# Eight small moves per batch in an attention and gated-convolution kernel: DMAs, or copies by GpSimd and VectorE

## The chip, the cores and the metric

One core of one Trainium2 chip. The time is the device time of one execution in microseconds (us). Most executions of one kernel agree closely; some fall into a slower state, which shows as runs more than 1.5% above the fastest of the same kernel. Such runs are left out of every ratio, but the medians quoted keep them. Ratios are the mean time of one kernel's fast runs over the mean of the other's fast runs in the same rounds on the same chip, so they are not quite the ratio of the medians that are quoted beside them. An interval is 95%.

## The reference

Eight batches, eight heads, 576 positions, head dimension 64. Attention is causal in blocks of 64; its result goes through a gated unit with a causal convolution over five positions.

```python
scores = q @ k.T / sqrt(64)                      # masked where block(i) < block(j)
attn   = exp(scores - max) / (sum + 1e-9)
x      = attn @ v                                # heads side by side: (8, 576, 512)
gate   = sigmoid(sum_k conv_w[k] * x shifted)    # five taps
out    = (gate * (x @ w_val)) @ w_out
```

## The kernel before

The kernel computes everything transposed, heads in pairs. Step `t` of the main loop holds the scores of one pair of heads of batch `t // 4`; older batches are interleaved with it. The denominators of a batch are summed by matmuls into one PSUM tile `dn`, head by head in rows of 32 partitions, and inverted in one instruction. The rows of `ri` then have to reach other partitions: a stream shuffle broadcasts one row within each group of 32 partitions (a quadrant), so each quadrant of `rq` first needs the rows of its own head, for both halves of the columns. `spread` does that with eight moves per batch.

```python
def den(b):
    dn = psG.tile([128, 9, 32], fp32, tag="G")
    ...                                                     # 69 to 72 matmuls
    ri = rp.tile([128, 288], fp32, tag="ri")
    nc.vector.reciprocal(out=ri[:, :], in_=dn[...])         # L257; L255 after the change

def spread(b):
    ri = ris.pop(b)
    for h in range(2):
        for u in range(2):
            for e in range(2):
                r0, r1 = 32 * (2 * h + u), 32 * (2 * h + e)
                move = nc.scalar.dma_start if b == 0 and h == 0 else load   # load: SyncE's queue
                move(out=rqs[b % 2][r0:r0 + 4, e, :], in_=ri[r1:r1 + 4, :])

def pv(t):
    rb = rp.tile([128, 2, 9, 32], fp32, tag="rb")
    nc.vector.stream_shuffle(out=rb[...], in_=rqs[b % 2][...], mask=[n] * 32)
    ...                                                     # x = v^T p, then xb = x * rb

def trans(hb, part):                                        # q and k of a later batch
    tr = psG.tile([128, 6, 128], fp16, tag="G")
    ...                                                     # six transposes by TensorE
    nc.vector.tensor_copy(out=qkT[b][...], in_=tr[...])     # L149; L147 after the change

def project(u, j):
    ot = psG.tile([128, 512], fp32, tag="G")                # four matmuls, then ob, then out
    ...
```

`psG` is a pool of four PSUM buffers that `dn`, `x`, `cv`, `tr`, `vp` and `ot` share in turn, so `ot` can start only when the `tr` four allocations earlier has been copied out. And only the matmuls and the loads are kept in program order; on VectorE, ScalarE and GpSimd a scheduler decides at build time in which order the instructions stand, and each engine then works through its list strictly in order.

The softmax here doesn't subtract the row's maximum and nothing guards it: scores larger than these inputs give would overflow.

## Time and profile before

| | before |
|---|---|
| median at first (3 runs, lowest to highest) | 257.14 us (255.12 to 259.04) |
| profiled execution, span | 255.2 us |
| TensorE busy | 219.8 us (86%), idle 31.4 us |
| VectorE, ScalarE, GpSimd busy | 57%, 54%, 36% |
| shuffles waiting for the small DMAs | 14.3 us in six places |

The busy line, the waits and the chain of one batch are shown in the prediction. The reading to keep: TensorE is the bound, so only idle time of TensorE can be won or lost; and in each batch there is a place where TensorE waits for two copies of `qkT` by VectorE with almost nothing to spare. The group of the projection's matmuls shows how small that wait is: after the bar, 144 matmuls had 0.5 us of idle time ahead of them in all.

```profile
L43 PE MATMUL ot<-w_out_sb,gv 128*128 128x512 f16 x144 | 35.8, 380 | 0.5
```

### The profile page before, as it was taken

The numbers are of one execution on the slowest core, as the hardware profiler recorded it, in microseconds if no ns is written. First come the engines' busy times: TensorE is split into PE (matmuls) and PEld (weight loads), VectorE is DVE, ScalarE is ACT, GpSimd is POOL, SyncE is SP. The second block draws the span as 40 slices with busy tenths as digits, with TensorE's granted clock in tenths as the row PEclk, the third lists the DMA queues.
The fourth block names the chain that finished last, engine by engine and source line by source line (L and its number), as shares of the span: only waits on it lengthen the run. The fifth ranks groups of instructions, "written<-read, shape, count | busy, mean of one in ns | idle before, by whom it ended". The sixth has DMA issues, their size and how long they took to land.

```text
span 255.2 us, 7299 instructions
## 1 busy us (share of the span) xinstructions
PE 219.8 (86%) x3064; PEld 152.2 (60%) x3064; DVE 145.8 (57%) x293; ACT 138.4 (54%) x233; POOL 92.4 (36%) x110
## 2 busy tenths in 40 slices
PE   0597869767999899999899989999999998999993
PEld 0374636645776467855675568655675567677661
DVE  2379952952787438652876457853766166366230
ACT  2459866255643675477554775376656761432533
POOL 7363963863943951454209240620027000000000
PEclk9999986798999999999999999999999999999999
DMA  6998787977398597059800992047101200230305
GB/s 190 342 298 203 247 231 150 300 242 184 100 286 183 184 355 188 5 154 383 229 5 11 356 296 69 7 148 205 44 4 47 92 33 4 89 125 3 154 13 205
DMA packets 25386, 40.62 MB, mean 159 GB/s; under 512 B 2053, under 2 KB 11525, under 8 KB 25354
## 3 DMA queue, kind: packets, MB, share of 16 engines
q1 hardware_dynamic: 20128, 30.69, 41.6%
q10 hardware_dynamic: 5226, 9.47, 9.9%
q8 instruction: 24, 0.39, 0.7%
q14 instruction: 8, 0.07, 0.1%
HBM read 30.42 MB, written 9.44 MB: 156 GB/s over the span
## 4 chain that ended last, share of the span: by engine, by line
PE 56%; ACT 18%; DVE 9%; issue 5%; DMA 5%; SPq 5%; ACTq 1%; DVEq 0%
PE cv L43 16%; ACT pt L178 15%; PE vp L43 9%; PE ps L43 8%; PE ot L43 7%; PE x L43 6%; PE dn L43 5%; PE tr L142 5%; SPq L46 5%; DVE qkT L149 4%; DVE ri L257 3%; DMA st<-in_k_dram 2%; ACT ob L366 2%; DMA rq_70<-ri 1%; DMA rq_71<-ri 1%
## 5 line engine op out<-in xcount | busy, mean ns | idle before, releaser
L178 ACT ACTIVATE pt<-ps 128x1024 f16<-128x1024 f32 (+1 forms) x96 | 76.0, 828 | 22.4 <-PE ps L43 19.5
L149 DVE COPY qkT<-tr 128x768 f16<-128x768 f16 (+1 forms) x62 | 49.2, 833 | 45.2 <-PE tr L142 45.1
L43 PE MATMUL ps<-qkT 64*64 64x64 f16 (+10 forms) x608 | 49.4, 253 | 17.7 <-ACT pt L178 14.2
L43 PEld LDWEIGHTS <-qkT 64*64 64x64 f16 (+1 forms) x608 | 24.7, 104 | 45.3 <-issue 38.1
L108 POOL CAST t<-st 128x1152 f16<-128x1152 f32 x30 | 34.3, 1145 | 33.3 <-DMA st<-in_q_dram 15.3
L338 ACT ACTIVATE th<-cv 128x288 f32<-128x288 f32 x64 | 26.1, 410 | 32.4 <-PE cv L43 30.8
L121 POOL CAST t<-st 128x2304 f16<-128x2304 f32 x8 | 16.9, 2106 | 67.2 <-PE x L43 50.8
L366 ACT COPY ob<-ot 128x512 f32<-128x512 f32 x36 | 21.3, 591 | 36.7 <-PE ot L43 33.3
L355 DVE SCALAR_TENSOR_TENSOR gv<-th,vp 128x288 f16<-128x288 f32 x64 | 26.8, 444 | 20.4 <-PE vp L43 19.9
L43 PE MATMUL ot<-w_out_sb,gv 128*128 128x512 f16 x144 | 35.8, 380 | 0.5
L43 PEld LDWEIGHTS <-diag 128*128 128x128 f16 x320 | 29.4, 98 | 10.0 <-issue 0.5
L142 PE MATMUL tr<-ident_59,t 128*128 128x128 f16 x288 | 26.9, 237 | 8.5 <-DVE ident_59 L82 6.7
L43 PE MATMUL x<-pt,t 128*64 128x256 f16 (+3 forms) x384 | 27.4, 255 | 2.7 <-DVE ri L257 2.0
L142 PEld LDWEIGHTS <-t 128*128 128x128 f16 x288 | 21.1, 106 | 12.4 <-DVE t L108 6.5
L204 ACT ACTIVATE pt<-ps 128x512 f16<-128x512 f32 x32 | 19.7, 615 | 15.0 <-PE ps L43 15.0
L43 PEld LDWEIGHTS <-w_val_sb 128*128 128x128 f16 x256 | 24.3, 98 | 5.4
L43 PEld LDWEIGHTS <-t 128*64 128x64 f16 x384 | 18.5, 112 | 6.7 <-issue 4.0
L43 PEld LDWEIGHTS <-gv 128*128 128x128 f16 x144 | 12.7, 97 | 14.8 <-issue 2.1
L257 DVE RECIPROCAL ri<-dn 128x288 f32<-128x288 f32 x8 | 15.7, 1958 | 8.3 <-PE dn L43 8.3
L43 PE MATMUL cv<-xb_67,diag 128*128 128x288 f16 x120 | 18.0, 299 | 0.2 <-DVE gv L355 0.2
L43 PE MATMUL cv<-xb_68,diag 128*128 128x288 f16 x120 | 16.8, 286 | 0.0
L43 PE MATMUL dn<-pt,oh 128*32 128x160 f16 (+7 forms) x704 | 14.1, 238 | 1.9 <-DVE xb_67 L316 1.9
(54 smaller groups left out, 223.5 us busy)
## 6 DMA issues: line engine op xcount, KB each, us to landing
st<-in_q_dram SPq DMA_DIRECT2D x32, 288.0 KB
st<-in_k_dram SPq DMA_DIRECT2D x32, 288.0 KB
out_dram<-ob ACTq DMA_DIRECT2D x36, 256.0 KB
st<-in_moe_w_val_dram SPq DMA_DIRECT2D x2, 512.0 KB
st<-in_moe_w_out_dram SPq DMA_DIRECT2D x2, 512.0 KB
rq_71<-ri SPq DMA_DIRECT2D x32, 4.5 KB
rq_70<-ri SPq DMA_DIRECT2D x28, 4.5 KB
st<-in_v_dram SPq DMA_DIRECT2D x8, 0.2 KB
```

Source lines behind the costliest of these rows:

```text
L43: tc.keep_in_program_order(nc.tensor.matmul(**kw))
L46: tc.keep_in_program_order(nc.sync.dma_start(**kw))
L108: cast(out=t[:, :, :, :], in_=st[:, :, :, :].rearrange("p z c d -> p c z d"))
L121: nc.gpsimd.tensor_copy(out=t[:, :, :], in_=st[:, :, :])
L142: tc.keep_in_program_order(nc.tensor.transpose(out=tr[:, s, :], in_=q16[hb, w][:, c, :, :], identity=ident16[:, :]))
L149: evac(out=qkT[b][:, 2 * half:2 * half + 2, w, :].rearrange("p n (x c) -> p n x c", c=9)[:, :, :, c0:c0 + len(ss)], in_=tr[:, ss[0]:ss[-1] ...
L178: nc.scalar.activation(out=pt[:, o:o + w], in_=src, func=AF.Exp, bias=0.0, scale=0.125)
L204: nc.scalar.activation(out=pt[:, 2048:2560].rearrange("p (h x) -> p h x", h=2), in_=ps[:, :, 0:256], func=AF.Exp, bias=0.0, scale=0.125)
L257: nc.vector.reciprocal(out=ri[:, :], in_=dn[:, :, :].rearrange("p j x -> p (j x)"))
L338: nc.scalar.activation(out=th[:, HF * hf:HF * hf + HF], in_=cv[:, :], func=AF.Tanh, bias=0.0, scale=0.5)
L355: nc.vector.scalar_tensor_tensor(out=gvs[u][:, g, c0:c0 + HF], in0=th[:, HF * hf:HF * hf + HF], scalar=1.0, in1=vp[:, :], op0=ALU.add, op1 ...
L366: nc.scalar.copy(out=ob[:, :], in_=ot[:, :])
```

## The change

The intent is to take the fixed cost of a DMA out of the path from reciprocal to shuffle: an on-chip copy of a whole quadrant moves the same rows. In batch 0 four of the eight are by VectorE; all others are by GpSimd. The memset of `rq` goes, as the copies now fill it.

```diff
-    for rq in rqs:
-        nc.gpsimd.memset(rq[:, :, :], 1.0)
...
-                    move = nc.scalar.dma_start if b == 0 and h == 0 else load
-                    move(out=rqs[b % 2][r0:r0 + 4, e, :], in_=ri[r1:r1 + 4, :])
+                    move = nc.vector if b == 0 and h == 0 else nc.gpsimd
+                    move.tensor_copy(out=rqs[b % 2][r0:r0 + 32, e, :], in_=ri[r1:r1 + 32, :])
```

## The prediction

> **What bounds the kernel now.** I read the page first: the engines, then the slices. TensorE is busy 86% and no other engine passes 57%.
>
> ```profile
> PE 219.8 (86%) x3064; PEld 152.2 (60%) x3064; DVE 145.8 (57%) x293; ACT 138.4 (54%) x233; POOL 92.4 (36%) x110
> ...
> PEclk9999986798999999999999999999999999999999
> ```
>
> The gaps of TensorE sum to 31.5 us, of which 9.4 lie before 12 us (first loads and casts). The rest are mostly repeated gaps of 0.41 us on the double-buffered score tiles, which this change does not touch. Three gaps look related to it: 1.65 us at 34.7, 1.88 us at 44.6, and 0.6 us in excess of the usual 0.41 at 84.0. So at most some 4 us can be won; the waits for the DMAs in the second fence are far larger in sum, but most of them are waits of an engine that is not the bound. The low PEclk digits (half clock in three stretches between 47 and 71 us) cost about 7 us and are not the change's business.
>
> Then the waits, for what the moved reciprocals hold up:
>
> ```profile
> DVE qkT L149 <- PE tr L142: 45.1, 23, 5.0
> ...
> POOL t L121 <- PE x L43: 50.8, 4, 22.3
> ...
> DVE rb L278 <- DMA rq_70<-ri: 8.5, 3, 3.6
> ...
> DVE rb L278 <- DMA rq_71<-ri: 5.8, 3, 3.4
> ```
>
> The shuffle (rb) waits 14.3 us in six places for the small DMAs: VectorE stands still there. GpSimd has long idle times: it runs ahead with its casts and waits for buffers.
>
> Last the chain of waits in one steady batch (the denominators of batch 5), which shows where VectorE is on the path:
>
> ```profile
> 157.28 1.56 PE dn L43 x70
> 158.85 0.02 issue
> 158.87 1.97 DVE ri L257
> 160.84 0.04 issue
> 160.88 0.64 PE x L43 x12
> 161.52 1.34 PE cv L43 x10
> 162.86 0.35 PE tr L142 x6
> 163.21 0.02 issue
> 163.24 0.52 DVE qkT L149
> 163.75 0.08 issue
> 163.83 0.72 DVE qkT L149
> 164.55 0.05 issue
> 164.59 1.05 PE ot L43 x4
> ```
>
> The output projection (ot) starts 0.05 us after the second qkT copy ends: it needs the PSUM buffer of the transposes, four allocations back in a pool of four. TensorE's previous work ends at 164.51, so there is only 0.08 us of slack: whatever delays these two copies delays TensorE.
>
> **What the Trainium skill says.** "GPSIMD Engine Reference", section 3.1: a simple GpSimd body runs at 1.03 cycles an element. The trace agrees: casts of 256, 1152 and 2304 columns took 398, 1145 and 2106 ns, which is 0.834 ns an element (1.00 cycle at 1.2 GHz) plus some 184 ns. The record alone misleads: "Perfetto Trace Analysis", section GPSIMD Engine Instruction, advises the spacing of starts. Consecutive 256-column casts start 0.345 us apart though each is recorded as 0.404, so the fixed part in a row is about 0.13 us. "DMA: Bandwidth & Descriptors", section on the anatomy of one DMA, gives about 2.0 us of fixed cost to a DMA, mostly the receipt of the write. The chain has 1.66 and 2.30 us from the last issue to the landing, plus 0.62 us for each issue. "Advanced Engine Details and Errata", Mode Summary: GpSimd and VectorE block each other when the Vector instruction uses both ports. The trace agrees: the 128x128 scalings (L379) took 238 ns alone and 1054 to 1281 ns when a GpSimd cast was running. The shuffles are not touched (800 ns without and 810 with GpSimd).
>
> **The change part by part.**
>
> *Removed:* 64 DMAs, 60 on SyncE's queue and 4 on ScalarE's, and two GpSimd memsets (1.2 us, at the start, where GpSimd then waits 4.67 us for the first load: nothing won). With the ScalarE DMAs go 0.58 to 0.70 us of issue each at 31.7 to 35.3 us. The exponential that TensorE waits for at 34.7 then starts about 1.1 us sooner (its scores are complete at about 34.3, it began at 35.31). With the SyncE DMAs goes the wait of 3.30 us of VectorE at 41.2 to 44.5, and TensorE's 1.88 us at 44.6 behind it. SyncE's loads no longer queue behind DMAs that wait for a reciprocal (7.4, 10.7 and 7.7 us blocked), but no TensorE gap after 12 us is put down to a late load, so I count nothing. At 83.5 us an output DMA on ScalarE's queue is held while the small DMAs are in flight; 0.6 us may go with them.
>
> *Added on VectorE, batch 0 only:* four 32x288 copies. They read and write SBUF in fp32, so they may use both ports, and at 33.8 us GpSimd is in the weight scaling (to 34.46) and then in its own four copies. I expect each to wait for the end of a GpSimd instruction: the four last some 1.9 us in place of about 0.9. VectorE has gaps of 0.94, 1.84 and 1.37 us there, so I charge 0.5 us.
>
> *Added on GpSimd:* 60 copies of 32x288. By the figures above one costs 184 + 288 x 0.834 = 424 ns by itself and 131 + 240 = 371 ns in a row; eight in a row take 7 x 0.371 + 0.424 = 3.02 us, plus 0.05 us for the semaphore: 3.07. That is 60 x 0.371 = 22 us more of GpSimd, which goes from 36% to some 44%: it does not become the bound. The casts behind the copies have slack of several steps of about 7 us.
>
> *Moved:* this decides it. Compared engine by engine, the instruction order of TensorE is the same, but on VectorE the scheduler has pulled the first shuffle of batches 2 to 6 ahead of the two qkT copies shown above (it stood five instructions later, and both shuffles together). VectorE works in order, so these copies now wait for eight GpSimd copies and a shuffle. For batch 5: the reciprocal ends at 160.83, the copies start at 160.88, end at 163.95, the shuffle starts at 163.98, and the next instruction 0.70 later (the spacing seen between two shuffles) at 164.68, in place of 163.24: 1.44 us late. The slack is 0.08 and existing waits of 0.05 remain, so TensorE loses about 1.4 us. Later in the batch VectorE gets this back (no wait of 1.07 us and one shuffle fewer at 167), but TensorE has no idle time there to return it. Batches 3, 4 and 6 have the same 2.40 us between the end of the reciprocal and the qkT copy; batch 2 has 2.6, so 1.2 us.
>
> *Sum:* 4 x 1.45 + 1.2 = +7.0 us; head -1.1 - 1.9 - 0.6 + 0.5 = -3.1 us. Batch 7 has the same hoist before its gating products: shuffle until 218.6 against a product that began at 217.42, 0.25 us late for a convolution at 219.95, but 0.19 us saved at 223.66: zero. Net +3.9 us on 257.14: **261.0 us**.
>
> **The rivals.**
> 1. *The win of the head and nothing else.* For it: the shuffles wait 14.3 us for DMAs, and a chain of eight issues (5 us) plus 2 us becomes 3.1 us. If the qkT copies had slack, or the GpSimd copies were done in under 1.7 us, the time would be 253 to 255 us. Against: the qkT copies end 0.05 us before the projection starts.
> 2. *GpSimd copies dearer than casts.* Nothing in this trace moves data between quadrants on GpSimd, and none has 32 partitions. At 0.55 us each a batch loses 1.3 us more: 5 x 1.3, so 267 us. Against: the cost fits columns alone, for 64 and for 128 partitions.
> 3. *GpSimd late for its copies,* because they stand behind casts that wait for loads and buffers, or the casts late behind the copies. Then transposes starve: some us more, 263 to 270. Against: GpSimd waits 7.7 to 22 us for a buffer in each batch from batch 3 on, and its queue reaches the copies with nothing open.
> 4. *VectorE and GpSimd share a port:* if shuffles were held by the copies, 32 x 0.4 us of VectorE. Against: 800 and 810 ns.
>
> **Range and chances.** The per-batch loss rests on a copy's spacing: 0.30 to 0.48 us gives a loss of 0.9 to 2.2 us, so +4.5 to +11 for five batches; the head gives -1.5 to -5. Runs of before spread from 255.1 to 259.0, and the half-clock stretches may fall elsewhere (2 us). That gives 256 to 266 us. The 2% line lies at 262.3, just above my value: slower by over 2% 0.37, within 2% 0.58, faster 0.05.
>
> **What would show it right or wrong.** Right: TensorE has a new gap of 1.2 to 1.6 us before ot in each of batches 2 to 6, put down to qkT, and just before it VectorE waits about 3 us less the x products for GpSimd's rq copies; the gaps at 34.7 and 44.6 us shrink; GpSimd is busy 112 to 118 us, the copies at 0.37 us spacing; the six waits of rb for DMAs are gone. Wrong: no gap before ot (then rival 1, the loss was hidden), copies at a spacing far from 0.37 us, the shuffle released by something other than rq, or the head unchanged because the VectorE copies or the load for the next transposes take the place of the waits removed.

## The result, and the profile after

The changed kernel is correct and slower: median 268.19 us (266.93 to 269.18, four runs) against 258.08 us (255.12 to 259.04, four runs, the upper two slow); ratio 1.047 (1.036 to 1.058). Repeated (run 10), the ratio was 1.039 (1.034 to 1.044). The predicted 261.0 us was too low, and the range of 256 to 266 us did not hold it.

The page of the changed kernel, engines and granted clock by slice:

```profile
PE 222.3 (84%) x3064; PEld 152.8 (58%) x3064; DVE 147.8 (56%) x297; ACT 138.7 (52%) x233; POOL 116.5 (44%) x168
...
PEclk9999988999897999999999999999999999999999
```

The span went from 255.2 to 265.1 us. TensorE's busy time grew by 2.5 us, its idle time from 31.4 to 38.9 us. GpSimd is at 44%, as predicted, and is no bound.

The waits of the changed kernel (engine and line, what released it: us in total, times, longest) name the place:

```profile
DVE rb L276 <- POOL rq_71 L267: 12.6, 4, 5.5
...
PE ot L43 <- DVE qkT L147: 10.5, 5, 2.1
...
DVE rb L276 <- POOL rq_70 L267: 7.1, 3, 2.4
...
PE x L43 <- DVE qkT L147: 3.5, 3, 2.6
...
PE ot L43 <- DVE gv L353: 1.3, 1, 1.3
```

The projection now waits five times, 10.5 us in all, each time for a `qkT` copy. The shuffles' waits for DMAs are gone, but they are not smaller: 12.6 + 7.1 = 19.7 us for GpSimd in place of 14.3 us for DMAs. The last two lines are waits of TensorE that the prediction did not have.

The chain of waits in the same batch as in the prediction (batch 5):

```profile
163.59 1.97 DVE ri L255
165.56 0.04 issue
...
167.46 0.42 POOL rq_71 L267
...
168.86 0.44 POOL rq_71 L267
...
169.33 0.03 DVE rb L276 x2
...
170.02 1.28 DVE qkT L147 x2
171.30 0.05 issue
171.34 1.05 PE ot L43 x4
```

The mechanism is the predicted one: copies, shuffle, `qkT`, `ot`. Its size is not. From the end of the reciprocal to the `qkT` copy there are 170.02 - 165.56 = 4.46 us; before it was 2.40. The copies start 0.46 us apart (at 167.46, 167.92, 168.39 and 168.86; two of them are in the cut), not 0.37, and the row of eight takes 3.67 us from 165.61 on, not 3.02.

TensorE issues the same 3064 matmuls in the same order in both kernels. So the start of the k-th matmul can be subtracted between two traces, and the difference shows where time is lost. This table, worked out so from the traces of the kernels named, gives the time lost against before (negative: won) in each stretch; the times are those of the kernel before, and the last four columns belong to experiments below.

| stretch of before | after | after again (run 10) | order pinned (run 1) | head alone (run 5) | one quadrant (run 9) |
|---|---|---|---|---|---|
| to 60.9 us: head, batch 0 | -4.62 | -2.45 | -5.91 | -4.35 | -4.13 |
| to 79.0: batch 1 | +3.13 | +1.45 | -0.22 | +1.87 | +1.49 |
| to 92.0: batch 2 | +2.15 | +2.33 | +1.60 | -0.58 | +1.56 |
| to 208.7: batches 3 to 6 | +8.13 | +10.66 | -0.03 | -0.02 | +6.16 |
| to the end: batch 7 | +1.12 | +1.12 | -0.35 | +0.03 | +0.46 |
| sum | +9.91 | +13.11 | -4.91 | -3.05 | +5.54 |

Each column is one profiled execution, and the clock of TensorE has a part in the first three rows. Up to the same matmul (60.9 us of before) the profile of before had 13.65 us at half clock, the others between 3.41 (after) and 13.65 us (run 9). And half clock in batch 1 shows in its row: in runs 2, 4, 7, 9 and 10 a stretch of it began between 59.3 and 61.5 us, and all five lose 1.44 to 1.49 us there; where none fell there and no gap opened (runs 1, 3, 6 and 8), 0.2 us is won.

In the changed kernel batches 3 to 6 lose 2.03, 2.04, 2.03 and 2.04 us, with no other difference between those matmuls: the gap of 2.12 us less the 0.08 us that was there before.

Batch 1 is another story. VectorE (start, duration, what, and in brackets the idle time before it and its releaser):

```profile
56.12 0.81 DVE L353 SCALAR_TENSOR_TENSOR gv<-th,vp 128x288 f16<-128x288 f32 x2
62.38 0.01 DVE L276 LOAD_MASK_SELECT rb<-rq_71  x1 [5.46 <-POOL rq_71 L267]
```

and GpSimd in the same time:

```profile
56.34 1.14 POOL L106 CAST t<-st 128x1152 f16<-128x1152 f32 x1
57.43 1.81 POOL L267 COPY rq_71<-ri 32x288 f32<-32x288 f32 x4
59.30 1.14 POOL L106 CAST t<-st 128x1152 f16<-128x1152 f32 x1
60.51 1.83 POOL L267 COPY rq_71<-ri 32x288 f32<-32x288 f32 x4
```

The reciprocals of batch 1 were ready at 48.33 us. GpSimd came to the copies at 57.43, after a row of casts and weight scalings without a break since 50.8, and put one more cast between the two halves. VectorE stood 5.46 us before the shuffle, both shuffles had been placed ahead of the `qkT` copies here, and TensorE lost 2.61 us at 62.5.

### The profile page after: what moved, and what is told of

Its sections match the earlier page's. It is cut to its first block, busy times and chain, and to the rows that moved or that the text cites.

```text
span 265.1 us, 7252 instructions
## 1 busy us (share of the span) xinstructions
PE 222.3 (84%) x3064; PEld 152.8 (58%) x3064; DVE 147.8 (56%) x297; ACT 138.7 (52%) x233; POOL 116.5 (44%) x168
## 4 chain that ended last, share of the span: by engine, by line
PE 60%; ACT 15%; DVE 8%; issue 6%; POOL 6%; DMA 3%; SPq 1%; POOLq 0%; ACTq 0%; DVEq 0%
PE cv L43 14%; ACT pt L176 12%; PE ps L43 11%; PE ot L43 9%; PE vp L43 9%; PE x L43 7%; PE tr L140 5%; PE dn L43 5%; DVE qkT L147 5%; DVE ri L255 3%; POOL rq_70 L267 3%; POOL rq_71 L267 3%; DMA st<-in_k_dram 2%; ACT ob L364 2%; DMA out_dram<-ob 1%
## 5 line engine op out<-in xcount | busy, mean ns | idle before, releaser
L43 PE MATMUL ps<-qkT 64*64 64x64 f16 (+10 forms) x608 | 51.2, 264 | 12.7 <-ACT pt L176 10.0
L43 PE MATMUL ot<-w_out_sb,gv 128*128 128x512 f16 x144 | 37.0, 388 | 12.0 <-DVE qkT L147 10.5
L140 PE MATMUL tr<-ident_59,t 128*128 128x128 f16 x288 | 27.6, 241 | 8.3 <-DVE ident_59 L82 6.4
L267 POOL COPY rq_71<-ri 32x288 f32<-32x288 f32 x32 | 13.5, 423 | 36.8 <-DVE ri L255 35.6
L267 POOL COPY rq_70<-ri 32x288 f32<-32x288 f32 x28 | 12.0, 427 | 32.9 <-DVE ri L255 31.9
L43 PEld LDWEIGHTS <-t 128*64 128x64 f16 x384 | 19.1, 113 | 10.4 <-issue 4.8
L43 PE MATMUL cv<-xb_67,diag 128*128 128x288 f16 x120 | 16.8, 286 | 0.0
```

Source lines behind the costliest of these rows:

```text
L43: tc.keep_in_program_order(nc.tensor.matmul(**kw))
L140: tc.keep_in_program_order(nc.tensor.transpose(out=tr[:, s, :], in_=q16[hb, w][:, c, :, :], identity=ident16[:, :]))
L267: move.tensor_copy(out=rqs[b % 2][r0:r0 + 32, e, :], in_=ri[r1:r1 + 32, :])
```

## The experiments

Theories at the start. A: the loss is the place of the shuffle in VectorE's list; the copies by themselves do no harm. B: the copies themselves, on GpSimd, disturb VectorE, the loads or the casts, wherever the shuffle stands. C: the copies are dearer than predicted, and the place is only the lever. A and C can both be partly true, so the tests of order come first, then those of the pace. Medians of before were 256.09 us in the first four runs and 257.33 in the next four, both on one chip, and 256.84 in the last two, on another.

**1. The order of before, the copies of after.** An ordering edge places each batch's shuffles behind the instruction that they followed before. Compared list by list, VectorE's order is then that of before, apart from the four copies of batch 0; the other engines have the order of the changed kernel.

```diff
...                                       # `last` notes each qkT copy and gating product
-        nc.vector.stream_shuffle(...)
+        behind = {1: (6, 2), 7: 23}.get(b, (2 * b + 3, 2))   # a qkT copy; in batch 7 a gating product
+        with tc.issue_after(last[behind].ins) if b else ExitStack():
+            nc.vector.stream_shuffle(...)
```

> The changed kernel with one thing undone: the shuffles of batches 1 to 7 are tied behind the qkT copies (or gating products) that they followed before the change, so VectorE's order is that of the kernel before but for the four copies of batch 0; all other engines keep the changed kernel's order, GpSimd copies included. Theory A (the hoisted shuffles hold up the qkT copies): the gaps before ot of 2.1 us in five batches, the 2.6 us at 62 us and 1.1 of the 1.3 us at 227 us go, 13.9 us in all: 268.2 - 13.9 = 254.3 us, some 4 us faster than before. Rival B (the GpSimd copies cost time by themselves, through shared ports or late casts): it stays at 263 or more. Rival C (half and half): 257 to 262.

Correct, median 252.4 us (252.13 to 254.67), ratio 0.987 (0.982 to 0.992). The whole loss is gone, and the kernel is 1.3% faster than before: less than the 2% that counts as faster here, but its interval lies below 1. VectorE in one batch of this kernel:

```profile
158.68 1.30 DVE L148 COPY qkT<-tr 128x384 f16<-128x384 f16 x2 [1.00 <-PE tr L141]
...
160.56 0.95 DVE L148 COPY qkT<-tr 128x768 f16<-128x768 f16 x1
161.43 0.02 DVE L279 LOAD_MASK_SELECT rb<-rq  x1
161.43 0.81 DVE L279 STREAM_SHUFFLE rb<-rq 128x576 f32<-128x576 f32 x1
```

The `qkT` copies run while GpSimd copies, and the shuffle then finds `rq` ready: no bracket, no wait. (In batches 2 and 7 it still waits, 1.25 and 0.19 us.) B has fallen: all 60 GpSimd copies are there, at the same pace, and batches 3 to 6 lose nothing (-0.03 us in the table). Not all of this run is explained by the change: the 1.60 us in the stretch of batch 2 is a gap of 2.02 us at 80.8, behind a ScalarE queue held by the issue of an output DMA until 81.63. Gaps of this kind (1.00 in before at 84.0, 2.25 in run 8 at 82.7, none in runs 2 and 5) come and go between kernels.

**2. The same for batches 2 to 6 alone.** The edge only where `2 <= b <= 6`.

> The same for batches 2 to 6 alone; batch 1 and batch 7 keep the hoisted shuffles. Theory A: only the five gaps of 2.1 us go (0.07 each stays), so 268.2 - 10.2 = 258.0 us, and the difference to the run with all batches tied is the 3.7 us of batch 1 and of the tail. If batch 1 and the tail are in truth free, it is equal to that run within 1 us.

Correct, median 255.25 us (253.12 to 257.81, the highest a slow run), ratio 0.994 (0.985 to 1.003): 2.8 us less than expected, and more than run 1, as expected. The five gaps before `ot` are gone. The tail's gap of 1.28 us stays, so it is the hoist in batch 7. Batch 1 was undecided: VectorE waited for late copies as in the changed kernel (the shuffle at 61.69), but TensorE stood only 0.26 us; its clock was halved from 59.3 to 62.7, so it was behind anyway, and the stretch still lost 1.44 us.

**3. The order of after, the DMAs of before.** The first shuffle of batches 2 to 6 is forced ahead of the `qkT` copies; the moves are the old DMAs. The cut leaves out that `spread` of these batches is called earlier and that one more edge keeps a gating product in its place.

```diff
-                    move = nc.vector if b == 0 and h == 0 else nc.gpsimd
-                    move.tensor_copy(...)
+                    move = nc.scalar.dma_start if b == 0 and h == 0 else load
+                    move(out=rqs[b % 2][r0:r0 + 4, e, :], in_=ri[r1:r1 + 4, :])
...
+        behind = last.get("x") if n == 0 else last.get((2 * b + 3, 2))   # x product; later qkT copy
+        with tc.issue_after(behind.ins) if n < 2 and 2 <= b <= 6 else ExitStack():
+            rbs[t] = rb, nc.vector.stream_shuffle(...)
...
+                front = rbs.get(2 * hb - 6)                              # the first shuffle
+                with tc.issue_after(front[1].ins) if front and part else ExitStack():
+                    nc.vector.tensor_copy(out=qkT[b][...], in_=tr[...])
```

> The kernel before with its DMAs, and only VectorE's order of batches 2 to 6 made that of the changed kernel (first shuffle ahead of the qkT copies; three ScalarE instructions also swap places). Theory A: each batch's qkT copies wait for the DMAs' landing and a shuffle; by the times in the trace before (shuffle start less qkT start, plus 0.70) that is 7.1, 4.8, 4.9, 4.6 and 5.1 us, 26 us in all: about 284 us, 278 to 286. Rival B (the engine and not the order): 258 us as before.

Correct, median 289.27 us (287.94 to 290.33), ratio 1.129 (1.124 to 1.134). The same place in batch 5:

```profile
DVE rb L284 <- DMA rq<-ri: 4.9, 1, 4.9
...
PE ot L43 <- DVE qkT L153: 4.7, 1, 4.7
```

Five gaps of 6.79, 4.89, 4.95, 4.67 and 4.70 us. Against the same order, the copies are a great gain; the order alone costs more than the whole change. The five stretches lost 33 us where the gaps sum to 26: the rest comes where stretches of half clock lie at the gaps (below).

**4. Half of the copies.** Only the four copies that cross quadrants, so half of `rq` keeps the ones of the old memset, which stays. Its output is wrong, which doesn't matter for the time. The second shuffle is pinned where the changed kernel has it.

```diff
-                for e in range(2):
+                for e in (1 - u,):
```

> The changed kernel with four copies a batch in place of eight (those that cross quadrants; wrong result on purpose), the second shuffle of batches 2 to 6 tied to its place. If the stall is the length of the row of copies at 0.464 us each, each of the five gaps falls by 4 x 0.464 = 1.86 us to about 0.25 us, the tail's goes and batch 1's gets 1 to 2 us shorter: 268.2 - 9.3 - 1.1 - 1.5 = 256.3 us. If a start-up cost before the first copy matters rather than their number: 264 or more.

Median 258.4 us (257.98 to 260.07), ratio 1.010 (1.006 to 1.014). The gaps before `ot` shrank from 2.1 to 0.32 to 0.35 us. Four copies fewer took 1.77 us off the gap. Had nothing else held the `qkT` copy, 4 x 0.464 = 1.86 us would have gone, so nearly the whole gap is set by the length of the row of copies. At the predicted 0.371 us the four would have been another 3 x 0.093 = 0.28 us shorter, which by this sum leaves almost no gap (an estimate; not run). That the time is 2 us above the 256.3 expected fits a gap that the copies did not make: 1.90 us at 122.9 in its trace, with half clock behind it, where 3.0 us was lost.

**5. The copies in batch 0 only.** Batches 1 to 7 go back to DMAs.

```diff
+                    if b == 0:
+                        move = nc.vector if h == 0 else nc.gpsimd
+                        move.tensor_copy(out=rqs[0][r0:r0 + 32, e, :], in_=ri[r1:r1 + 32, :])
+                    else:
+                        load(out=rqs[b % 2][r0:r0 + 4, e, :], in_=ri[r1:r1 + 4, :])
```

> Batch 0 by copies as in the changed kernel, batches 1 to 7 by DMAs as before; VectorE's order is that of the kernel before but for the four copies. The part of the win that belongs to the head: TensorE's gaps of 1.65 us at 34.7 and 1.88 us at 44.6 fall to 0.4 and 0, some 3.1 us: about 253 us where before is 256.1. If it gives as much as the run with all copies and the order tied back (0.987), the copies of batches 1 to 7 win nothing by themselves; if it gives nothing, the win is theirs.

Correct, median 253.74 us (253.49 to 254.0), ratio 0.989 (0.985 to 0.994), about 2.7 us. That is the same as run 1 within the intervals, so batch 0 alone gives as much as all the copies with the order pinned, as far as times can tell. It does not follow that the copies of the other batches win nothing. In this run's trace the shuffle of batch 1 waits for its DMAs, and TensorE for the product behind it:

```profile
65.65 0.01 DVE L281 LOAD_MASK_SELECT rb<-rq  x1 [1.91 <-DMA rq<-ri]
67.59 1.39 PE L43 MATMUL cv<-xb,diag 128*128 128x288 f16 x10 [1.78 <-DVE xb L319]
```

That is its +1.87 us in the table. Run 1, with copies there, has no such gap, but it has the gap of 2.02 us in batch 2 that this run lacks; so the equal totals are in part chance. In batch 7 the copies win 0.35 us (runs 1, 7 and 8; 0.03 us is lost here). Only in batches 3 to 6 do copies and DMAs come to the same in the order of before (-0.03 and -0.02 us). No run has copies in batches 0 and 1 alone, so what those of batch 1 are worth stays open.

**6. The pace by itself.** Batch 0 as after; in batches 1 to 7 eight GpSimd copies go to a tile that nobody reads, each batch with another kind of row, to find what makes the copies start 0.46 us apart where casts start 0.345 apart. Its output is wrong, which doesn't matter for the time.

```diff
+                    q0, q1, p = {1: (q, q, 32), 2: (0, 0, 32), 3: (0, q, 32), 4: (q, 0, 32),
+                                 5: (q, 32 * (k // 2), 32), 6: (0, 0, 128), 7: (0, 0, 64)}[b]
+                    nc.gpsimd.tensor_copy(out=pace[q0:q0 + p, k, :], in_=ri[q1:q1 + p, :])
```

Here `k` counts the eight copies and `q` is 32 times `k % 4`; `q0` and `q1` are the first partitions of output and input.

> Eight GpSimd copies a batch into a tile that nobody reads, a different kind in each batch (wrong result on purpose); only their spacing counts. Theory S (a change of the starting partition from one GpSimd instruction to the next costs the overlap): batch 2 (all in quadrant 0), batch 6 (128 partitions) and batch 7 (64 partitions) at 0.37 us, batches 1, 3, 4 and 5 (in, out or both change quadrant) at 0.46 us. Theory Q (crossing quadrants inside a copy costs it): batches 1, 2, 6 and 7 at 0.37, batches 3 to 5 partly at 0.46. Theory W (four-byte results or 32 partitions cost it): all at 0.46, or all but 6 and 7.

One run, of unknown state; only the spacing counts. Eight copies as one group, first the row of batch 2 (all from and to the first quadrant), then that of batch 3 (to the first, from changing ones):

```profile
73.93 3.01 POOL L277 COPY pace<-ri 32x288 f32<-32x288 f32 x8
```

```profile
101.50 3.64 POOL L277 COPY pace<-ri 32x288 f32<-32x288 f32 x8 [9.19 <-DVE ri L258]
```

Same shape and type, 3.01 against 3.64 us. From the starts: 0.370 us apart in batches 2, 6 and 7 (32, 128 and 64 partitions from partition 0), 0.458 to 0.466 in batches 1, 3, 4 and 5. Batch 1 copies within a quadrant but changes the quadrant from copy to copy: slow. So it is neither the crossing, nor fp32, nor the number of partitions. What costs 0.09 us is that an instruction's first partition, of input or output, differs from that of the instruction before it: the two then don't overlap (each is recorded as about 0.42 us, longer than 0.370 and shorter than 0.458). The quadrants were the only steps tried.

The trace of before held this already. Its casts of `v` start at partition 0 or 64 by turns: of the rows without a break on GpSimd, 36 instructions start at the partition of the one before, and all begin 0.02 to 0.06 us before that one ends; 26 start at another, and all begin 0.04 to 0.09 us after it ends.

**7. All eight copies on VectorE.** `move = nc.vector` in every batch, order left to the scheduler.

> All eight copies of every batch on VectorE, in the scheduler's own order (five of them ahead of the two qkT copies, three behind). No wait for another engine is left. If a copy takes its undisturbed 0.28 us, the qkT copies come 0.3 us late in each batch: 254 us. If the copies wait for GpSimd instructions that run at the time, as in batch 0 (a cast of 2.1 us, one of 1.0 and then 0.35 each), the qkT copies are some 2.4 us late in most batches: 260 to 265 us.

Correct, median 273.46 us (271.89 to 274.3), ratio 1.066 (1.058 to 1.073); I had expected 260 to 265 us. VectorE in batch 5, then GpSimd:

```profile
171.23 3.96 DVE L267 COPY rq<-ri 32x288 f32<-32x288 f32 x5
175.21 1.28 DVE L147 COPY qkT<-tr 128x384 f16<-128x384 f16 x2
```

```profile
170.59 2.11 POOL L119 CAST t<-st 128x2304 f16<-128x2304 f32 x1 [9.73 <-PE x L43]
172.63 1.11 POOL L121 CAST d<-st 64x1024 f16<-64x1024 f32 x1
173.79 1.66 POOL L123 CAST d<-st 64x256 f16<-64x256 f32 x4
```

One such copy takes 0.30 us where GpSimd is idle. Here five took 3.96 us: 1.62, 1.04, 0.43, 0.41 and 0.41, each about as long as the cast that ran beside it had left or took (in batches 3 and 4 up to 2.14, over parts of two casts). GpSimd's long cast kept its 2.11 us; the shorter ones grew by some 0.07 us (1.11 in place of 1.03, 0.47 in place of 0.40). The gaps before `ot` were 0.53, 4.80, 4.80, 2.95 and 3.00 us. This fits the block of the shared port that the prediction cites, and it fell almost wholly on VectorE.

**8. All eight on GpSimd, order pinned.** Run 1 with `move = nc.gpsimd` in batch 0 too.

> The order tied back as in the first run, and batch 0's eight copies all on GpSimd, so no VectorE copy meets a GpSimd cast. The four VectorE copies took 2.3 us in batch 0 where VectorE has slack: no change is expected against the first run's ratio of 0.987, within 0.5%. If the batch 0 copies on VectorE cost TensorE time, up to 1 us is won.

Correct, median 253.52 us (252.99 to 254.29), ratio 0.989 (0.984 to 0.994). Like run 1: which engine makes the four copies of batch 0 does not matter here.

**9. The changed kernel with one starting partition.** Same order on every engine as the changed kernel (but for two memsets at the start), same number of copies of the same shape, but all from and to partitions 0 to 31, into a larger tile of which the shuffle reads what the last two copies wrote. Its output is wrong, which doesn't matter for the time.

```diff
-                    move.tensor_copy(out=rqs[b % 2][r0:r0 + 32, e, :], in_=ri[r1:r1 + 32, :])
+                    move.tensor_copy(out=rqs[b % 2][0:32, 4 * h + 2 * u + e, :], in_=ri[0:32, :])
```

> The changed kernel with every instruction in the same place on every engine, but all eight copies read and write quadrant 0 (wrong result on purpose), so that they follow each other every 0.37 us as the prediction assumed. The five gaps before ot should be 2.11 - 7 x 0.093 = 1.46 us, which is the prediction's 1.4, the tail's gap 0.65 us shorter: some 4 us less than the changed kernel of the same rounds (1.5%). If the pace of the copies does not carry through to the gap, the two are equal.

Median 262.11 us (260.56 to 263.89), ratio 1.022 (1.015 to 1.028). The row of copies of batch 5:

```profile
163.23 3.02 POOL L269 COPY rq<-ri 32x288 f32<-32x288 f32 x8 [9.12 <-DVE ri L257]
```

3.02 us is the prediction's own figure for the row, and the gaps in batches 3 to 6 are 1.46, 1.46, 1.46 and 1.45 us, against 1.45 predicted. Batch 2 had 2.22 us, as a cast delayed its first copy from 74.5 to 75.31. In the table each of batches 3 to 6 loses 1.37 or 1.38 us (the remaining 0.66 is a chance gap at 125.5), 0.65 less than in the changed kernel; and 7 x (0.464 - 0.371) = 0.65. By the medians the kernel is 5.4 us faster than run 10, where 4 were expected; the five gaps and the tail account for 3.9, and the half clock that run 10 has at its gaps (below) may be the rest.

**10. The changed kernel again.**

> The changed kernel itself, beside the run above on the same chip: 1.047 of the kernel before, gaps of 2.1 us before ot in batches 2 to 6.

Correct, median 267.47 us (266.39 to 271.32, six runs, the highest a slow one), ratio 1.039 (1.034 to 1.044). The five gaps are 2.11 to 2.12 us and the tail's 1.30 us as at first; in batch 1 there is no large gap; TensorE was at half clock there (61.5 to 64.9), and the stretch loses 1.45 us as in the other runs with half clock there. The granted clock by slice, of this run and then of run 9:

```profile
PEclk9999989977997999889997999979999999999999
```

```profile
PEclk9996599977999999999999999999999999999999
```

In this run, whose slices are 6.7 us long, four dents follow after 80 us (7, 88, 7 and 7); run 9 has none there. In the trace they are stretches of 3.41 us at half clock, and four of the five gaps of 2.1 us are followed by one; in the first run of the changed kernel only one of five was. The loss of batches 3, 4 and 5 rises by 0.81, 0.92 and 0.81 us with it.

## Why the prediction was wrong, point by point

The prediction had +3.9 us; the profiled pair has +9.9. Its terms, beside the first column of the table:

| term | predicted | measured | verdict |
|---|---|---|---|
| head | -1.1 - 1.9 + 0.5 = -2.5 | -4.6 (run 10 -2.5) | right in kind; the size moves with the clock |
| batches 3 to 6 | 4 x 1.45 = +5.8 | +8.1 | mechanism right, size wrong |
| batch 2 | +1.2 - 0.6 = +0.6 | +2.2 | the same, with half clock behind the gap |
| batch 1 | not counted | +3.1 (run 10 +1.5) | missed |
| batch 7 | 0 | +1.1 | missed |
| sum | +3.9 | +9.9 | |

The prediction put its -0.6 us for the gap at 84 us under the head; it lies in batch 2 and is moved there (runs 2 and 5 win 0.58 us in that stretch).

1. *What moves.* The step "VectorE works in order, so these copies now wait for eight GpSimd copies and a shuffle" is shown: pinning the order takes the whole loss away (run 1), and the hoist without the copies makes a larger one (run 3). TensorE did not win it back later, as predicted.

2. *The term that was mis-sized* is "131 + 240 = 371 ns in a row; eight in a row take 7 x 0.371 + 0.424 = 3.02 us". It took the overlap from four casts that start at the same partition, and gave it to copies that change theirs each time; other casts of the same trace, which change theirs, do not overlap. The copies start 0.464 us apart and the row takes 3.67 us. Run 6 shows the cause, and run 9, which takes only this away, has the predicted row and the predicted gap. That is 0.65 us in each of five batches, 3.3 us of the 6.0 us that the profiled pair lies above the prediction. It is not all: run 9, with the row as predicted, still loses 5.5 us in its trace in place of 3.9. (In its working for batch 5 the prediction counts 0.05 us twice, at 160.88 and in 3.07; that alters nothing else.) Rival 2 of the prediction, dearer copies, was the right one, at 0.46 in place of 0.55 us; the argument against it ("the cost fits columns alone") concerned the length of one instruction, not what follows it.

3. *Batch 1* was left out of the sum: the comparison of orders had shown that its shuffles moved ahead of `qkT` copies too, and I took only batches 2 to 6. Rival 3, "GpSimd late for its copies", was put aside because GpSimd has long waits "in each batch from batch 3 on"; batch 1 lies before that, and there the copies came 9 us after the reciprocals. Of its 3.1 us TensorE's idle time makes 1.95 (4.26 against 2.31 us in that stretch); the other 1.2 us is longer busy time, with a stretch of half clock right behind the gap (65.1 to 68.5 us). In the runs with half clock ahead of it (2, 9 and 10) the gap is hidden and half clock alone goes with 1.4 to 1.5 us. So the loss by the order is shown for one profile, and its mean is not known.

4. *Batch 7* was called zero, from 0.25 us late against 0.19 us saved. With the row 0.65 us longer the lateness grows to 0.9 us; the gap was 1.30 and the loss 1.1. Run 9 with the short row still had a gap of 0.64 and lost 0.46. The reader was the wrong one: the prediction looked at the convolution at 219.95, but what waits for the product is the fourth matmul of a projection, which ran at 218.29 before, 0.42 us after the product ended.

5. *The clock.* I gave the half-clock stretches 2 us of the range, as chance that is the same for both kernels. The gaps seem to attract them: of gaps of 2.9 us and more in runs 3 and 7 all nine had half clock begin in the gap or within 1.4 us of its end, of those of 2.07 to 2.12 us in the two runs of the changed kernel five of ten, of three others of 2.02, 2.25 and 2.22 us (runs 1, 8 and 9) none, and of the four of 1.46 us in run 9 none; but one of 1.90 us (run 4) and the one of 2.61 us in batch 1 had it, one of 1.78 us (run 5) not. This is an association over few gaps; run 9 comes nearest to changing the gap alone, and its gaps have no half clock, but neither had four of the five in the first profile. What each costs is 0.8 to 0.9 us in batches 3 to 5 of run 10, and about 1.7 us in batch 1 (1.44 lost with it, 0.22 won without). At these rates for 3.41 us the 13.65 us of before cost some 3 to 7 us (an estimate); the prediction's 7 us is the upper end. (The stretches in the profile of before lay at 35.9 to 59.8 us from the span's start; the 47 to 71 in the prediction were read from the time base of the raw trace, which starts 11.2 us earlier.)

The 64 DMAs and their 14.3 us of waits were the intent of the change. Taking all of them away is worth about 3 us when the order is kept (runs 1 and 8), and taking those of batch 0 away 2.7 us (run 5). That batch 0 is a cause shows in TensorE's idle time after 12 us and up to the end of the head: 8.72 us before, 8.53 in run 3 with the old DMAs, 4.05 to 5.27 in the ten traces with copies in batch 0. What stays open: why the clock follows one gap of 2.1 us and not the next, and how much of the head's -2.5 to -5.9 us in different runs is its half-clock stretches rather than the change. (Runs 4 and 9 had the 13.65 us of half clock of before in the head and were still 3.7 and 4.1 us sooner; run 3 was 2.1 us sooner at 10.24 us.)

The fastest median is that of run 1, 252.4 us where before took 256.09; runs 5 and 8 are equal to it within the intervals, and run 5 has the fewest copies.

## What to carry to other kernels

A wait that shows in the profile is worth only what it holds up on the engine that bounds the kernel; look for that before replacing the transfer behind it. When a producer becomes quicker, a scheduler may move its consumer forward: compare the lists engine by engine, look at what now stands behind the waiting instruction, and pin the order where that is on the path. Take the time of a row of instructions from rows of the same kind, down to the partitions where they start (the profile at hand may hold such rows), and check every place that moved, not only the steady ones.

## What the Trainium skill lacked or had wrong

- "GPSIMD Engine Reference" says nothing of rows of instructions whose first partitions differ. Measured: 32x288 fp32 copies start 0.370 us apart when input and output start at the same partition as in the instruction before, 0.458 to 0.466 us when either changes (run 6); in the kernel that made 3.67 us of a row of eight in place of 3.02 (run 9), and casts in the trace of before show the same. "VectorE: DVE Perf Modes", section "Two Vector instructions with no wait between them", describes such a rule, as a model (an instruction is held until all earlier ones have finished when the quadrant where its input or output starts is not that of the one before), for VectorE only; GpSimd behaved as if it had the same.
- "TensorE: Matmul & The Clock Gate", Part 1, puts the return to half clock after an idle window of about 3.4 us. The half-clock stretches last 3.41 us or two or three times that. But half clock came at gaps shorter than such a window: at five of ten gaps of 2.1 us in the changed kernel and at one of 1.90 us in run 4, and at none of four gaps of 1.46 us.
